# A hand-written issue order laid out anew: linear attention followed by a gated long convolution, on one core

## The chip, the cores and the metric

The kernel runs on one core of one Trainium2 chip. The metric is the device time of one execution in microseconds (us); three executions of the kernel before took 242.75, 243.77 and 244.01 us, so its median is 243.77 us. All computing engines of the core take part: TensorE (PE in the profile; PEld is its weight load), VectorE (DVE), ScalarE (ACT), GpSimd (POOL) and SyncE (SP), the last of which only issues transfers here.

## The reference

For each of 8 batches (b), 8 heads (h), 576 positions (s) and 64 channels (d), with inputs `q`, `k`, `v` of 9.4 MB each in float32:

```
kv  = einsum('bhsd,bhse->bhde', k, v)
out = einsum('bhsd,bhde->bhse', q, kv)
x   = out / sqrt(mean(out*out, -1) + 1e-6) * g_norm        # rows of 8*64 = 512 channels
x1, x2, x3 = split(x @ w_proj, 3)                          # each 576 x 512
x2c = irfft(rfft(x2, axis=time) * rfft(filter_fft, axis=time))
result = (x1 * x2c * x3) @ w_out                           # float32, (8, 576, 512)
```

## The kernel before, in words

Matrix operands are bfloat16 (the loads convert), sums are float32 in PSUM. The 576-point transform is done by matmuls with cosine and sine tables that the kernel makes itself. The sequence is folded into sums and differences first, so that short tables do.

**Steps.** The body is a set of named steps, and each step issues the instructions of one engine for one batch, with few exceptions. These are the ones that the text speaks of.

- Loads on POOL's queue: `Lq`, `Lk`, `Lv` bring one batch of an input (line 100; with `a` or `b` behind the name, half the heads), `Lf` the filter (L248), `Lw1`, `Lw2`, `Lw3`, `Lwo` the weights (L109). Input buffers are double.
- Set-up, once: `Z`, `Zi`, `Zt`, `Zf` make constants, `An0` to `An2` the tables `IV` (L176 to L183), `Tb0` to `Tb2` transpose them on PE, `Ff0` to `Ff2` fold the filter (L261, L263), `H0` to `H2` make the filter's spectrum `HH`, `HM` (L278 to L293), with ScalarE and VectorE taking turns. `Act` loads ScalarE's function table (L190). `W0_` to `W15_` are fillers: they put 4 matmuls on nothing (10 for `W0_`, L79) ahead of the next step that takes PSUM.
- Attention: `K` and `eK` make the kv blocks (L313, L319). `T0`, `T1` transpose q on PE for batches 0 and 1 (L340); from batch 2 on, `Qt` does that with a transposing DMA on SP's queue (L333). For each quarter j of the channels, `Oj` multiplies (L376), `sqj` squares and `obj` (or `ovj` on VectorE) scales out of PSUM (L386, L393, L391), `Rj` sums over a head (L383), `rsj` takes the inverse root (L397). `x0`, `x1` form the normalised x (VectorE, L409).
- Transform: `fd`, `fa`, `fr` fold x (VectorE, L420 to L434). `abM`, `abT`, `rrM`, `rrT` project the folded x by the middle third of w_proj (PE, L464, L471, L450, L457), `eab`, `eT`, `err` bring that to SBUF (ACT, L475). `F0`, `F1`, `F2` are the forward transform (L488 to L505).
- Product with the spectrum: `M0` and `M1` are two multiplications each on VectorE, a PSUM operand by an SBUF one, float32 into the SBUF tile `tpw` (L511, L512). `M2` is one (L527). Then the two halves of a complex product are added, both operands in SBUF: `Av1` on VectorE for group 1, `A0` on GpSimd for group 0 (both L518).
- Gates: for each quarter dc, `Gadc` and `Gbdc` project x by the first and last third of w_proj (PE, L537), `x1dc` copies the one out (ACT, L543), `gdc` multiplies the two (VectorE, L545).
- Inverse: `Io` and `I` for quarters 01 and 23 (PE, L561, L562; they read all that M2, A0 and Av1 of the batch wrote), `os` (ACT, L565), `u` (VectorE, L570, L571), `w` (L577 to L579), `fin` (L582, the product with the gates).
- Output: `U0`, `U2` and, every other batch, `U4` multiply by w_out (L609, L622), `ot0`, `ot2`, `ot4` copy out (ACT) and store with four DMAs each on SP (L616, L629). The last batch uses `V0` to `V3` (L641) with `va`, `vv` (L645, L648), in place of U0 and U2. Three output tiles are used in turn.

**What sets the order.** The kernel turns the framework's scheduler off: the written order of the steps is the order of each engine's queue. Three strings hold it. FIRST is done once, then ROUND for r = 0 to 6, then LAST. A `+` behind a step means the batch after r (`++` the second after), a `-` the one before; a step that was done already is left out. So a round runs a software pipeline: attention of batch r+2, transform and gates of batch r+1, the inverse's end of batch r and the output of batch r-1.

**PSUM.** There are four pairs of banks. `take` gives a step the pair that was freed longest ago in the written order, and the engine then waits until the step that freed it has really been done:

```
def take(key, n=2):
    i = min(range(4), key=lambda x: seen[x])
...
def free(key):
    seen[held.pop(key)] = clock[0]
```

So the written order sets not only the queues, it also sets which copy out of PSUM each matmul group waits for.

Of the kernel before, what the change touches and what calls it, by code (L numbers as in the profile page):

```python
# [16 lines left out]
MAGIC = 3.0 * (2.0 ** 22)  # L17


FIRST = """Lq Z Lkb Zi Zt An0 An1 An2 Zf Lf W0_ T1 W1_ Tb1 Tb0 Lvb Tb2 W10_ Ff0 T0 Lka Kb eTv1 Lva eKb O3 sq3 eTv0 Ff1 ov3 Ff2 O2 Ka  # L20
sq2 Act Lq+ W6_ R2 eKa ov2 rs2 W7_ O0 O1 Lk+ sq0 ov0 sq1 W8_ R3 rs3 W9_ H0 x1 R0 Lv+ rs0 W2_ W3_ T0+ W11_ R1 Lw2 ov1 eTa0+ rs1 fr1 fd1 x0
H1 fd0 T1+ fa0 fa1 fr0 K+ eK+ Lw1 H2 eTa1+ W4_ O0+ abM W5_ abT eab O1+ rrM eT F1 sq0+ sq1+ Lw3 rrT ob0+ Ga0 ob1+ err
M1 x10 R0+ Lwo F0 R1+ Ga1 rs0+ rs1+ x11 O2+ Gb0 Lv++ sq2+ Av1 F2 M0 ob2+ O3+ sq3+ Lq++ Gb1 g0 A0 ob3+ R2+ R3+
M2 rs2+ g1 x0+ Gb2 rs3+ x1+ Io01 os01 I01 Ga2 fd+ fa+ x12 Ga3 abM+ u01 g2 abT+ Gb3 w01 eab+ eT+ fr+ F1+ Io23
x13 rrM+ os23 g3 Lk++ rrT+ M1+ I23 F2+ u23 err+ F0+ M0+ w23 fin23 fin01"""

ROUND = """fd+ I23 fa+ Lq+++ Qt++ os23 fr+ ot0- Gb3 abM+ g3 rrM+ u23 K++ rrT+ eab+ U4- eK++ err+ w23 ot4- abT+ Ga1+ eT+
x11+ O3++ O2++ sq3++ sq2++ Lv+++ fin23 w01 ob3++ F1+ fin01 ob2++ U2- F0+ Ga0+ ot2- R2++ M1+ Gb0+ x10+ rs2++
M0+ O1++ Ga2+ g0+ sq1++ Av1+ ob1++ x12+ F2+ Lk+++ R3++ A0+ rs3++ O0++ Gb1+ M2+ sq0++ x1++ R1++ Gb2+ ob0++ g1+
rs1++ R0++ Io01+ g2+ rs0++ I01+ Ga3+ os01+ x0++ x13+ u01+ Io23+ U0"""  # L30

LAST = """os23 w01 ot0- I23 Gb3 U2- fin01 ot2- u23 g3 w23 fin23 U4 ot4 V3 V1 vv3 vv1 V0 V2 va2 va0"""


@with_exitstack
def kernel(
# [629 lines left out]
    def do(words, r):  # L666
        for word in words.split():
            n = word.rstrip("+-")
            b = r + word.count("+") - word.count("-")
            if 0 <= b < B and b in only.get(n, range(B)) and (n, b) not in did:  # L670
                clock[0] += 1
                step[n](b)
                did.add((n, b))

    do(FIRST, 0)
    for r in range(B - 1):
        do(ROUND, r)
    do(LAST, B - 1)

# [29 lines left out]
```

## Time and profile before

The profiled execution took 242.64 us; its span, from the first to the last instruction, is 240.9 us. So 1.7 us lie around the span, and the execution is 1.1 us below the median of 243.77 us.

| engine | busy, us | share of the span | instructions |
|---|---|---|---|
| PE | 215.6 | 89% | 1897 |
| VectorE | 203.5 | 84% | 323 |
| ScalarE | 150.8 | 63% | 236 |
| GpSimd | 45.9 | 19% | 55 |

The chain of waits that ended last is 60% PE and 26% VectorE. The granted TensorE clock is 0.991 over the span. Transfers move 30.14 MB, 125 GB/s on average, about 200 GB/s in the first 40 us.

How to read this: a share of busy time is an average over the start (to about 66 us), seven rounds of some 24 us, and the end. Within a round PE and VectorE are both almost always busy, so the question for any step is which of the two the other waits for at that place. A wait that several semaphores share is named after the one that came last.

### The profile page before, as it was taken

To read this page: it belongs to the slowest core of one execution; us is meant where nothing else is said; L and a number is where in the kernel's file an instruction comes from. 1 tells how busy PE (TensorE), PEld (TensorE's weight loads), DVE (VectorE), ACT (ScalarE), POOL (GpSimd) and SP (SyncE) were. 2 spreads that over 40 slices of the span, in tenths; PEclk is the share of its full clock that TensorE was granted. 3 is DMA by queue.
4 is the path that set the end of the run, shared out by engine and by line. 5 is a ranking of instruction groups with operands and counts; after the bars stand their busy time and mean duration, and the time that the engine had idled before them with its cause. 6 is when DMAs were issued, how large, how long until landed. Compare 5 with 4: busy or idle time off the path is not lost.

```text
span 240.9 us, 4753 instructions
## 1 busy us (share of the span) xinstructions
PE 215.6 (89%) x1897; PEld 126.6 (53%) x1897; DVE 203.5 (84%) x323; ACT 150.8 (63%) x236; POOL 45.9 (19%) x55
## 2 busy tenths in 40 slices
PE   7599997999979999799979997999799979997970
PEld 2354442466446755575547555755475557465520
DVE  3946288399999999999899999997999999999930
ACT  2648566884569558756875597568855875532421
POOL 7732000035043000700070007000300030003021
PEclk9999999999999999999999999999999999999996
DMA  5999999507999932997299819992703120430184
GB/s 47 198 198 204 206 206 176 102 1 105 203 185 135 162 90 44 167 189 171 68 171 189 186 35 175 172 191 64 165 3 87 24 65 1 104 93 25 42 214 140
DMA packets 41193, 30.14 MB, mean 125 GB/s; under 512 B 16050, under 2 KB 36530, under 8 KB 41170
## 3 DMA queue, kind: packets, MB, share of 16 engines
q0 software_dynamic: 21200, 17.11, 47.3%
q1 hardware_dynamic: 19778, 12.46, 22.6%
q8 instruction: 15, 0.25, 0.4%
q10 hardware_dynamic: 192, 0.26, 0.3%
q14 instruction: 8, 0.07, 0.1%
HBM read 33.69 MB, written 9.44 MB: 179 GB/s over the span
## 4 chain that ended last, share of the span: by engine, by line
PE 60%; DVE 26%; DMA 5%; ACT 3%; issue 2%; SPq 1%; ACTq 0%; DVEq 0%; POOLq 0%
PE ps L537 16%; PE ps L609 9%; DVE Y L518 8%; PE ps L464 4%; PE ps L561 4%; PE ps L79 3%; DVE Y L527 3%; DMA qb<-in_q_dram 3%; DVE g L545 3%; PE ps L471 3%; PE ps L450 3%; DVE tpw L512 2%; PE ps L313 2%; DVE tpw L511 2%; DMA out_dram<-ot 2%
## 5 line engine op out<-in xcount | busy, mean ns | idle before, releaser
L537 PE MATMUL ps<-x,wp 128*128 128x288 bf16 x512 | 72.7, 286 | 7.0 <-DVE Y L527 6.5
L537 PEld LDWEIGHTS <-wp 128*128 128x128 bf16 x512 | 47.3, 97 | 25.5 <-issue 11.6
L518 POOL TENSOR_TENSOR Y<-tpw 97x1024 bf16<-97x1024 f32 x8 | 18.8, 2352 | 164.4 <-DVE tpw L512 164.4
L475 ACT CAST x<-ps 128x1024 bf16<-128x1024 f32 (+1 forms) x24 | 20.6, 874 | 17.2 <-PE ps L464 14.7
L397 ACT ACTIVATE rstd<-ps,bias_eps 128x576 bf16<-128x576 f32 x32 | 23.8, 746 | 9.9 <-PE ps L383 9.8
L543 ACT CAST x<-ps 128x576 bf16<-128x576 f32 x32 | 20.5, 642 | 11.9 <-PE ps L537 10.3
L609 PE MATMUL ps<-wo,yg 128*128 128x512 bf16 x112 | 26.5, 379 | 0.0
L511 DVE TENSOR_TENSOR tpw<-ps,HH 128x1024 f32<-128x1024 f32 (+1 forms) x16 | 19.6, 1222 | 7.8 <-PE ps L498 7.2
L545 DVE TENSOR_TENSOR g<-ps,x 128x576 bf16<-128x576 f32 x32 | 23.3, 746 | 0.1
L386 ACT ACTIVATE sq<-ps 128x576 bf16<-128x576 f32 x32 | 20.0, 656 | 2.4 <-PE ps L376 2.3
L518 DVE TENSOR_TENSOR Y<-tpw 128x1024 bf16<-128x1024 f32 x8 | 20.6, 2571 | 0.0
L393 ACT ACTIVATE o<-ps,g_col 128x576 bf16<-128x576 f32 x28 | 20.1, 752 | 0.0
L79 PE MATMUL ps<-kvblk,ind 128*128 128x512 bf16 x54 | 16.5, 445 | 3.9 <-DVE ind L145 1.6
L512 DVE TENSOR_TENSOR tpw<-ps,HH 128x1024 f32<-128x1024 f32 (+1 forms) x16 | 19.4, 1214 | 0.0
L613 ACT COPY ot<-ps 128x1024 f32<-128x1024 f32 x14 | 14.2, 1015 | 7.6 <-PE ps L609 5.5
L561 PE MATMUL ps<-IV,Y 128*128 128x192 bf16 x128 | 16.5, 245 | 1.5 <-DVE Y L527 0.9
L609 PEld LDWEIGHTS <-yg 128*128 128x128 bf16 x112 | 10.6, 98 | 11.4
L565 ACT COPY os<-ps 128x576 f32<-128x576 f32 x16 | 10.2, 635 | 8.3 <-PE ps L562 5.7
L464 PE MATMUL ps<-wp,ab 128*128 128x512 bf16 x64 | 15.1, 379 | 0.0
L383 PE MATMUL ps<-sq,ind 128*128 128x288 bf16 x64 | 13.1, 286 | 0.8 <-ACT o L393 0.6
L409 DVE TENSOR_TENSOR x<-o,rstd 128x1152 bf16<-128x1152 bf16 x16 | 12.0, 750 | 1.5 <-ACT rstd L397 1.5
L561 PEld LDWEIGHTS <-Y 128*128 128x128 bf16 x128 | 10.3, 98 | 5.6 <-DVE Y L527 1.0
(135 smaller groups left out, 344.2 us busy)
## 6 DMA issues: line engine op xcount, KB each, us to landing
out_dram<-ot SPq DMA_DIRECT2D x56, 128.0 KB, 2.3
qb<-in_q_dram POOLq DMA_DIRECT2D x8, 576.0 KB, 8.1
kb<-in_k_dram POOLq DMA_DIRECT2D x7, 576.0 KB, 13.3
vb<-in_v_dram POOLq DMA_DIRECT2D x7, 576.0 KB, 10.3
wp<-in_moe_w_proj_dram POOLq DMA_DIRECT2D x3, 512.0 KB, 18.7
out_dram<-ot SPq DMA_DIRECT2D x24, 64.0 KB, 1.7
kb<-in_k_dram POOLq DMA_DIRECT2D x2, 288.0 KB, 9.1
fn<-in_moe_filter_fft_dram POOLq DMA_DIRECT2D x1, 576.0 KB, 8.4
```

Source lines behind the costliest of these rows:

```text
L79: nc.tensor.matmul(pair[i][:, 0], ind, kvblk[1].rearrange("p a b c -> p (a b c)"), start=True, stop=True)
L397: act.activation(out=by_time(rstd(), j), in_=by_row(tmp['r', b, j]), func=AF.Abs_reciprocal_sqrt, scale=1.0 / D, bias=bias_eps)
L464: nc.tensor.matmul(pp[:, h], abt()[:, j, h * SB:h * SB + P], w2(j), start=(j == 0), stop=(j == NDC - 1))
L475: act.copy(out=o_(), in_=tmp[key, b])
L511: vec.tensor_mul(out=t_[:n, 0], in0=xp[:n], in1=HH[:n, g, 1:3])
L512: vec.tensor_mul(out=t_[:n, 1], in0=xp[:n], in1=HH[:n, g, 0:2])
L518: op(out=Yt()[:n, 2 * g:2 * g + 2], in0=t_[:n, :, 0], in1=t_[:n, :, 1])
L537: nc.tensor.matmul(pp[:, h, 0:TH], w_, x[:, j, h * TH:(h + 1) * TH], start=(j == 0), stop=(j == NDC - 1))
L543: act.copy(out=x1, in_=pp[:, :, 0:TH])
L545: vec.tensor_mul(out=halves(g13t()[:, dc]), in0=pp[:, :, 0:TH], in1=x1)
L561: nc.tensor.matmul(pp[:, i, 0:SB], Y[:, 2 * g + h, cs], IV[:, 2 * g + h, 0:SB], start=(g == 1), stop=(g == 2))
L609: nc.tensor.matmul(pp[:, cc], ygt(b)[:, dc, c * P:(c + 1) * P], wo[:, dc], start=(dc == 0), stop=(dc == NDC - 1))
```

## The change

Only the three strings are changed; no step is added or altered, except that fewer fillers are named (W0, W1, W2, W6 to W9 and W12 in place of W0 to W11). In the set-up, the filter's load goes ahead of k and v, both transposes of q ahead of the tables, `Act` ahead of `Zt`, and `F0` with `M0` of a batch comes before `M1` in batch 0 and 1. In a round, `A0` is written behind `M0` and ahead of `M2`, `g0`, `g1` and `Av1`. In LAST the final inverse follows the last gates.

```
-ROUND = """fd+ I23 fa+ Lq+++ Qt++ os23 fr+ ot0- Gb3 abM+ g3 rrM+ u23 K++ rrT+ eab+ U4- eK++ err+ w23 ot4- abT+ Ga1+ eT+
-x11+ O3++ O2++ sq3++ sq2++ Lv+++ fin23 w01 ob3++ F1+ fin01 ob2++ U2- F0+ Ga0+ ot2- R2++ M1+ Gb0+ x10+ rs2++
-M0+ O1++ Ga2+ g0+ sq1++ Av1+ ob1++ x12+ F2+ Lk+++ R3++ A0+ rs3++ O0++ Gb1+ M2+ sq0++ x1++ R1++ Gb2+ ob0++ g1+
-rs1++ R0++ Io01+ g2+ rs0++ I01+ Ga3+ os01+ x0++ x13+ u01+ Io23+ U0"""
+ROUND = """K++ Lk+++ x0+ Qt++ U0- Lq+++ x13 eK++ fd+ Io23 u01 O2++ fa+ Gb3 fr+ ot0- Lv+++ os23 I23 abM+ g3 sq2++ u23
+ob2++ rrM+ eab+ abT+ rrT+ eT+ U4- O1++ w01 err+ ot4- sq1++ ob1++ O3++ sq3++ fin01 ob3++ F1+ U2- w23 fin23 F0+
+ot2- M1+ Ga1+ x11+ F2+ Ga0+ M0+ Gb0+ x10+ A0+ R3++ M2+ O0++ Gb1+ g0+ R2++ rs3++ Ga2+ g1+ sq0++ Av1+ ob0++
+rs2++ R0++ x1++ Gb2+ x12+ R1++ rs0++ rs1++ g2+ Ga3+ Io01+ os01+ I01+"""
...
-LAST = """os23 w01 ot0- I23 Gb3 U2- fin01 ot2- u23 g3 w23 fin23 U4 ot4 V3 V1 vv3 vv1 V0 V2 va2 va0"""
+LAST = """u01 Io23 x13 U0- I23 w01 U2- os23 u23 fin01 ot0- Gb3 w23 ot2- g3 fin23 V2 V1 U4 va2 vv1 V3 V0 ot4 vv3 va0"""
```

FIRST, before and after:

```
-FIRST = """Lq Z Lkb Zi Zt An0 An1 An2 Zf Lf W0_ T1 W1_ Tb1 Tb0 Lvb Tb2 W10_ Ff0 T0 Lka Kb eTv1 Lva eKb O3 sq3 eTv0 Ff1 ov3 Ff2 O2 Ka
-sq2 Act Lq+ W6_ R2 eKa ov2 rs2 W7_ O0 O1 Lk+ sq0 ov0 sq1 W8_ R3 rs3 W9_ H0 x1 R0 Lv+ rs0 W2_ W3_ T0+ W11_ R1 Lw2 ov1 eTa0+ rs1 fr1 fd1 x0
-H1 fd0 T1+ fa0 fa1 fr0 K+ eK+ Lw1 H2 eTa1+ W4_ O0+ abM W5_ abT eab O1+ rrM eT F1 sq0+ sq1+ Lw3 rrT ob0+ Ga0 ob1+ err
-M1 x10 R0+ Lwo F0 R1+ Ga1 rs0+ rs1+ x11 O2+ Gb0 Lv++ sq2+ Av1 F2 M0 ob2+ O3+ sq3+ Lq++ Gb1 g0 A0 ob3+ R2+ R3+
-M2 rs2+ g1 x0+ Gb2 rs3+ x1+ Io01 os01 I01 Ga2 fd+ fa+ x12 Ga3 abM+ u01 g2 abT+ Gb3 w01 eab+ eT+ fr+ F1+ Io23
-x13 rrM+ os23 g3 Lk++ rrT+ M1+ I23 F2+ u23 err+ F0+ M0+ w23 fin23 fin01"""
+FIRST = """Z Lq Lf Zi Lka Act Zt Lva An0 An1 An2 Lvb W0_ T1 Zf T0 eTv0 eTv1 Tb0 Lkb Lq+ Lw2 Ff2 Ff0 Tb2 Ff1 W2_ Ka eKa W1_ Tb1 O1 sq1
+ov1 O0 sq0 R0 rs0 W6_ R1 Kb eKb rs1 ov0 O2 sq2 ov2 W7_ O3 Lk+ R2 sq3 R3 rs2 x0 rs3 ov3 x1 Lv+ fr1 T0+ fr0 T1+ eTa0+
+Lw1 eTa1+ H2 H0 rrM fd0 rrT fa0 fd1 err fa1 W8_ H1 F0 W9_ abM eab K+ M0 eK+ abT O2+ eT sq2+ O0+ F2 sq0+ F1 ob2+ Lw3
+ob0+ O3+ M2 sq3+ Lwo ob3+ M1 R2+ Ga0 Lq++ rs2+ Ga1 R3+ R0+ x10 Gb0 x11 O1+ A0 Av1 rs3+ rs0+ g0 Gb1 sq1+ ob1+
+Lk++ R1+ x1+ Ga3 Ga2 g1 Io01 rs1+ Gb3 x13 Lv++ x0+ fr+ x12 os01 I01 rrM+ rrT+ fd+ fa+ g3 err+ abT+ eT+ Io23
+u01 os23 I23 abM+ F0+ eab+ Gb2 F2+ u23 M0+ F1+ g2 M1+ w23 fin23 w01 fin01 K++ Lk+++ Qt++ Lq+++ eK++ W12_ O2++"""
```

## The prediction

> **What bounds the kernel now.** I read the page's busy times first, then the timeline of one round engine by engine, then the stages one by one, then the end.
>
> ```profile
> PE 215.6 (89%) x1897; PEld 126.6 (53%) x1897; DVE 203.5 (84%) x323; ACT 150.8 (63%) x236; POOL 45.9 (19%) x55
> ...
> DVE  3946288399999999999899999997999999999930
> ```
>
> PE and VectorE are both nearly full from 46 us on, so neither share says which one rules. The timeline of one round does:
>
> ```profile
> 119.70 1.21 DVE L512 TENSOR_TENSOR tpw<-ps,HH 97x1024 f32<-97x1024 f32 x1
> 120.83 0.75 DVE L545 TENSOR_TENSOR g<-ps,x 128x576 bf16<-128x576 f32 x1
> 121.50 3.02 DVE L518 TENSOR_TENSOR Y<-tpw 128x1024 bf16<-128x1024 f32 x1
> 124.44 1.21 DVE L527 TENSOR_TENSOR Y<-ps,HM 128x1024 bf16<-128x1024 f32 x1
> ```
>
> ```profile
> 121.09 2.35 POOL L518 TENSOR_TENSOR Y<-tpw 97x1024 bf16<-97x1024 f32 x1 [19.98 <-DVE tpw L512]
> ```
>
> ```profile
> 125.71 1.14 PE L537 MATMUL ps<-x,wp 128*128 128x288 bf16 x8 [1.27 <-DVE Y L527]
> ```
>
> GpSimd's sum (A0) starts 0.18 us behind M0's second product and runs to 123.44. VectorE's sum (Av1) starts at 121.50 and takes 3.02 us; its end, 124.52, is A0's end and 1.08 us. M2 (L527) follows late, and PE waits 1.27 us for the pair that M2 frees (Gb2). That is PE's only marked gap of a round. The first batch shows each piece alone:
>
> ```profile
> 48.64 1.22 DVE L518 TENSOR_TENSOR Y<-tpw 128x1024 bf16<-128x1024 f32 x1
> ...
> 52.05 0.74 DVE L545 TENSOR_TENSOR g<-ps,x 128x576 bf16<-128x576 f32 x1
> 52.72 1.21 DVE L527 TENSOR_TENSOR Y<-ps,HM 128x1024 bf16<-128x1024 f32 x1
> ...
> 69.75 2.44 DVE L578 TENSOR_TENSOR w<-u,w 128x384 bf16<-128x384 bf16 x1
> ```
>
> ```profile
> 52.22 2.36 POOL L518 TENSOR_TENSOR Y<-tpw 97x1024 bf16<-97x1024 f32 x1 [28.59 <-DVE tpw L512]
> ```
>
> Av1 without A0 takes 1.22 us. A0 beside products that read PSUM (52.05, 52.72) takes the same 2.36 us, and these take their usual 0.74 and 1.21. The next A0 (batch 1) hits L578, whose two inputs lie in SBUF: 2.44 us, where its median is 0.36. So A0 stops VectorE's work from two SBUF operands, not its PSUM products.
>
> **A round, worked out.** Rounds last 23.79 us, 24.58 with U4 (stage table, from U2 to U2):
>
> ```profile
> 115.88:139.67 23.79, 22.51 (x212) 13.97 (x211) 22.86 (x31) 16.60 (x27) 4.62 (x4) 1.00 0.83 151
> 139.67:164.25 24.58, 23.30 (x219) 14.36 (x218) 22.87 (x31) 17.40 (x28) 4.61 (x4) 1.00 0.83 146
> ```
>
> The columns are length, then busy PE, PEld, DVE, ACT, POOL. PE is busy 22.51 and idle 1.28. In the new order VectorE does M1, M0, M2, g0, g1, Av1. A0 starts 0.18 us behind M0 and needs 2.35 us; M2, g0 and g1 take 1.13 + 0.67 + 0.67 = 2.47 us start to start. So Av1 meets at most 0.1 us of A0 and falls from 3.02 to 1.22, and VectorE's load falls by 1.8 to 21.05 us. Av1's unknown price lies between 1.22 and 3.02; I take 1.22, because the order leaves A0 only PSUM products as company.
>
> What is late next? I walked the new order with these durations, time 0 being K's start. PE has K 0.78, U0 1.73, Io23 0.43, O2, Gb3, I23, abM 1.73, rrM 0.95, abT 0.96, rrT, O1, O3 and so on; F1 starts at 9.2, U2 10.06, F0 11.8, Ga1 12.4, F2, Ga0, Gb0 15.05, Gb1 16.55, Ga2 17.85, Gb2 19.15, Ga3, and the inverse ends at 22.3. The releases come before each: eT 9.0 for F1, err 9.95 for U2, ob3 12.2 for Ga1, M1 13.0 for Ga0, M2 16.5 for Gb1, g1 18.4 for R0, rs0 20.3 for Io01. VectorE's own loop, from rs1 over x0, fd, u01, fa, fr, g3, u23, w01, fin01, w23, fin23, M1, M0 and M2 (17.3 us), then Gb1 to R1 on PE (4.1) and rs1 (0.75), is 22.2 us, with hand-overs 22.3. So PE's 22.5 rules, by a margin of 0.2 us only. I take 1.2 us saved in each of the five rounds that show the full wait (101.1 to 197.9): **6.0**, with ends 3.0 (half goes to hand-overs) and 6.4. In batch 7 PE waits 0.60 and 0.88 us for Av1 and M2 (220.1, 221.2); in the new order ten gate groups lie between F1 and Io01, and Av1 is done 1 us early: **1.3** saved (1.0 to 1.5).
>
> POOL's three loads stand ahead of A0; they are issued right behind the last A0, wait for nothing that is late, and land in 8.1 to 13.4 us (medians), while their readers come over 20 us later. Qt is moved behind ot2's stores on SP, see the rivals.
>
> **The start.** Up to I01 of batch 1 I walked the order in the same way. q lands at 9.03 before, with half of k behind it; now the filter (576 KB) is second. At the rates of the transfer rows q lands between 9.0 and 10.6 us; I take 9.1, as the rows show q done when 0.81 MB had moved. Both transposes (12 take 1.14 us cold) end at 11.4, the angle tables at 11.6 as before, and Tb0, Ff2, Ff0, Tb2, Ff1 and Ka follow to 17.3. From there the two orders compare so (us):
>
> | | before, row | after, worked out |
> |---|---|---|
> | x complete for batch 0 | 34.7 | 27.5 |
> | first spectrum product (M1, now M0) | 46.25 | 38.7 |
> | Ga0 of batch 0 | 46.7 | 44.8 |
> | K of batch 2 | 67.2 | 61.9 |
> | M2 of batch 1 | 76.1 | 68.6 |
> | I01 and Ga3 of batch 1 done | 80.5 | 75.6 |
>
> What moves the first product is the H steps: with ScalarE and VectorE taking turns at 1.5 us per pair, they come when x is folded already, and F0 needs only the rr part. The gain shrinks again, since VectorE then waits some 4 us for F2, Gb0, Gb1 and F0. My hops are about 0.09 us short each (an O group starts its square 0.36 us after its own start, I counted 0.25 and 0.1), on some 14 hops of the path: 1.2 us. So **3.7** of the 4.9 remain. Ends: 0 (q at 10.6 and twice the hop error) and 5.5. Hidden costs: two more function table loads (1.28 each) run before ScalarE's first input at 4.3 us; the one ahead of rs0 takes the place of the one at 21.91. The 16 fillers taken away are 0.22 us each when warm, and lay in gaps.
>
> **The end.** From I01 of batch 7 to the last fin is 6.85 us before (222.97 to 229.82). After, VectorE has only g2 beside Io01 and os01, so the path is os01, u01, w01, u23, fin01, w23, g3, fin23: 7.6 us, **0.75 lost**. Behind fin the stores take 11.1 us now (to 240.9); with V2 and V1 ahead of U4, and the last tile waiting only for V1's stores, I get 10.4: **0.7 gained**, uncertain by 1 us either way.
>
> **Sum.** 6.0 + 1.3 + 3.7 - 0.75 + 0.7 = 10.95 us of the profiled 242.64, so 231.7 for that execution; the median lies 1.1 above it: **232.8 us**.
>
> **Rivals.**
>
> *Hand-overs eat the round* (0.13). The margin of 0.2 us is thin, as the next release is late wherever one copy is. Half of the rounds' gain (3.0), 1.3, and 2 of the start: 6.3 saved, 237.5 us. For it: both loops are within 1%. Against: the old order shows no gap but one.
>
> *A0 still meets Av1* (0.06), so the change doesn't do what it says: if POOL's loads hold A0 back by 2 us, Av1 waits as now and only the start pays, 240.1, or 243.8 if that gives nothing either (half each). Against: POOL shows no wait before its loads in the rounds.
>
> *Qt comes late* (0.07), the slower side. Now Qt is issued at 121.20 or 144.56 and its readers, the O matmuls, run 17 to 18 us later (138.36, 163.08). In the new order Qt follows ot2's stores (15.9 in the round before), and O2 of that batch is at 2.9: 9.3 us later. It takes 5.1 us to land, 8.5 at most. From 9.3 us on PE, in order, stops at O2 with Gb3, I23 and abM behind it, and each further us counts in five rounds. At 3 us beyond, 15 us are lost against 11 gained: 248 us. For it: k, q and v of the next batch are issued 2 us behind it and share the transfer engines. Against: that was so before.
>
> *PE falls to its slow pitch in the start* (0.04). Four fillers take 1.91 us at 9.98 and 1.04 at 14.66, so PE was slow until about 12 us, after an idle stretch of 3 us. My walk leaves no gap over 1.4 us after that. If one slow stretch of 2.9 us came back, half of it is lost: 234.2. The Trainium skill, "TensorE: Matmul & The Clock Gate", section "What's actually happening", says that an idle window of about 3.4 us takes the clock to half, which speaks against dropping fillers; by the gaps of my walk it would not happen.
>
> *The forecast* has 0.70, its own range 229.4 to 235.5.
>
> **Range and chances.** The low end takes all upper ends (6.4, 1.5, 5.5 and +1 at the end: 229.4). The high end takes in the hand-over case with nothing from the start and a worse end: 238.5. About 0.5% (1.2 us) is what a measurement can tell from no change. Faster: 0.70 + 0.13 + 0.04 + 0.03 = 0.90; same: 0.03; slower: 0.07.
>
> **What would show it.** Av1 at 1.2 us in every round, A0 beside L527 and L545; no PE wait for L527; rounds of 22.5 to 22.7 (23.3 with U4); M0 of batch 0 near 40; the span behind fin23 near 10.4 us. Wrong if PE shows waits over 0.3 us for L475, L527 or Qt's data in each round, or if the first product comes after 45 us.

## The result and the profile after

The new kernel takes 232.47 us (median of four executions, 230.74 to 234.36), the kernel before, run beside it, 243.26 us (242.37 to 244.01). The ratio is 0.953, with a 95% interval of 0.945 to 0.962. The profiled execution took 231.38 us, with a span of 229.6. A ratio compares undisturbed executions only, so it need not be the quotient of the two medians.

The page of the new kernel, busy times and VectorE's tenths:

```profile
PE 209.0 (91%) x1860; PEld 126.4 (55%) x1881; DVE 191.7 (83%) x323; ACT 152.3 (66%) x238; POOL 45.8 (20%) x55
...
DVE  4864587789898999899889998998899989998920
```

VectorE lost 11.8 us of busy time with the same 323 instructions, so single instructions became shorter: 10.9 us of it is Av1, whose eight instances took 20.6 us before and take 9.7 now. The timeline of one round shows which (VectorE, then GpSimd; columns as before: start, duration, engine, line, operation):

```profile
91.25 1.22 DVE L512 TENSOR_TENSOR tpw<-ps,HH 97x1024 f32<-97x1024 f32 x1
92.38 1.22 DVE L527 TENSOR_TENSOR Y<-ps,HM 128x1024 bf16<-128x1024 f32 x1
93.67 0.76 DVE L545 TENSOR_TENSOR g<-ps,x 128x576 bf16<-128x576 f32 x1
95.18 0.76 DVE L545 TENSOR_TENSOR g<-ps,x 128x576 bf16<-128x576 f32 x1 [0.75 <-PE ps L537]
95.86 1.22 DVE L518 TENSOR_TENSOR Y<-tpw 128x1024 bf16<-128x1024 f32 x1
```

```profile
92.64 2.35 POOL L518 TENSOR_TENSOR Y<-tpw 97x1024 bf16<-97x1024 f32 x1 [24.11 <-PE ps L537]
94.94 0.79 POOL L100 DMA_DIRECT2D kb<-in_k_dram  x1
```

A0 now runs from 92.64 to 94.99, beside M2 and g0. Av1 starts behind it, at 95.86, and takes 1.22 us instead of 3.02. Two rounds of the new kernel, each from one F2 to the next (length, then busy PE, PEld, DVE, ACT, POOL); measured so, the rounds of the kernel before are 24.59 and 23.78 us:

```profile
90.79:113.95 23.16, 23.05 (x218) 14.59 (x218) 21.22 (x32) 17.22 (x27) 4.61 (x4) 1.00 0.87 160
113.95:136.25 22.30, 22.19 (x210) 14.14 (x210) 21.05 (x32) 16.62 (x26) 4.63 (x4) 1.00 0.90 155
```

A round is 1.44 to 1.48 us shorter, and PE is now busy in all but 0.11 us of it. So PE bounds the rounds, and the wait for L527 is gone from them.

Where the 11.3 us of span went (240.9 less 229.6), at the same places in both traces:

| stretch | before | after | saved | predicted |
|---|---|---|---|---|
| start, until I01 and Ga3 of batch 1 are through PE | 80.48 | 77.21 | 3.27 | 3.7 |
| from there to the same of batch 7 | 142.49 | 133.35 | 9.14 | 6.0 + 1.3 |
| from there to fin23's end | 6.85 | 7.70 | -0.85 | -0.75 |
| from fin23's end to the span's end | 11.1 | 11.34 | -0.25 | +0.7 |

The table compares one execution of each kernel. The rounds repeat to 0.02 us in the other profile of the new kernel, but the first row is 2.8 us larger there and the last 0.8 us smaller (see the slow pitch and the end, below).

### The profile page after: what moved, and what is told of

Same layout as the page of the kernel before. It is cut to its first block, busy times and chain, and to the rows that moved or that the text cites. A ratio compares the mean times of both kernels' runs of the same rounds, so it can differ in the third digit from the quotient of the medians.

```text
span 229.6 us, 4731 instructions
## 1 busy us (share of the span) xinstructions
PE 209.0 (91%) x1860; PEld 126.4 (55%) x1881; DVE 191.7 (83%) x323; ACT 152.3 (66%) x238; POOL 45.8 (20%) x55
## 4 chain that ended last, share of the span: by engine, by line
PE 72%; DVE 15%; ACT 6%; issue 2%; DMA 2%; POOL 1%; ACTq 0%; DVEq 0%; POOLq 0%
PE ps L537 26%; PE ps L609 9%; PE ps L464 5%; PE ps L561 4%; PE ps L383 3%; PE ps L471 3%; PE ps L450 3%; PE ps L313 2%; PE ps L376 2%; PE ps L261 2%; PE ps L505 2%; PE ps L497 2%; DMA out_dram<-ot 2%; PE ps L457 1%; PE ps L490 1%
## 5 line engine op out<-in xcount | busy, mean ns | idle before, releaser
L537 PE MATMUL ps<-x,wp 128*128 128x288 bf16 x512 | 71.3, 286 | 0.6 <-ACT o L393 0.5
L537 PEld LDWEIGHTS <-wp 128*128 128x128 bf16 x512 | 49.0, 98 | 17.1 <-issue 1.1
L545 DVE TENSOR_TENSOR g<-ps,x 128x576 bf16<-128x576 f32 x32 | 24.0, 754 | 5.3 <-PE ps L537 5.1
L386 ACT ACTIVATE sq<-ps 128x576 bf16<-128x576 f32 x32 | 21.0, 662 | 1.7 <-PE ps L376 1.7
L511 DVE TENSOR_TENSOR tpw<-ps,HH 97x1024 f32<-97x1024 f32 (+1 forms) x16 | 19.5, 1220 | 2.0 <-PE ps L498 1.3
L393 ACT ACTIVATE o<-ps,g_col 128x576 bf16<-128x576 f32 x28 | 21.1, 758 | 0.0
L512 DVE TENSOR_TENSOR tpw<-ps,HH 97x1024 f32<-97x1024 f32 (+1 forms) x16 | 19.4, 1215 | 0.0
L561 PE MATMUL ps<-IV,Y 128*128 128x192 bf16 x128 | 16.2, 245 | 0.0
L565 ACT COPY os<-ps 128x576 f32<-128x576 f32 x16 | 10.3, 642 | 7.1 <-PE ps L562 6.1
L570 DVE TENSOR_TENSOR u<-ps,os 128x576 bf16<-128x576 f32 x16 | 12.0, 750 | 1.8 <-ACT os L565 1.8
L562 PE MATMUL ps<-IV,Y 97*128 97x96 bf16 x64 | 13.2, 207 | 0.0
L79 PE MATMUL ps<-kvblk,ind 128*128 128x512 bf16 x35 | 11.5, 452 | 1.8 <-DVE ind L145 1.6
```

The costliest lines, as they stand in the source:

```text
L386: act.activation(out=halves(sq()[:, j]), in_=tmp['o', b, j][:, :, 0:TH], func=AF.Square)
L393: act.activation(out=by_time(osb(), j), in_=i_, func=AF.Copy, scale=g_col)
L511: vec.tensor_mul(out=t_[:n, 0], in0=xp[:n], in1=HH[:n, g, 1:3])
L537: nc.tensor.matmul(pp[:, h, 0:TH], w_, x[:, j, h * TH:(h + 1) * TH], start=(j == 0), stop=(j == NDC - 1))
L545: vec.tensor_mul(out=halves(g13t()[:, dc]), in0=pp[:, :, 0:TH], in1=x1)
L561: nc.tensor.matmul(pp[:, i, 0:SB], Y[:, 2 * g + h, cs], IV[:, 2 * g + h, 0:SB], start=(g == 1), stop=(g == 2))
```

## The experiments

### Is it A0 beside a sum of two SBUF operands?

The new kernel with one step moved: Av1 directly behind M2, so in the middle of A0.

```
-... M0+ Gb0+ x10+ A0+ R3++ M2+      O0++ ... Ga2+ g1+ sq0++ Av1+ ob0++
+... M0+ Gb0+ x10+ A0+ R3++ M2+ Av1+ O0++ ... Ga2+ g1+ sq0++      ob0++
```

> The new kernel with Av1 written right behind M2 in the rounds, ahead of g0 and g1, so that it falls into the middle of A0. Theory (A0 stops VectorE's work from two SBUF operands, and keeping them apart is what the rounds gained): Av1 takes about 2.5 us (1.4 us of waiting for A0 and 1.1), g0 comes 2 us late, PE's R2 waits for g0's pair by about 2 us in each of six rounds, total about 243 to 245 us. Rival (the gain comes from the new order of the PSUM releases, A0 does not matter): Av1 stays at 1.22 us, R2 waits about 0.6 us, total 235 to 237 us.

Measured: 244.46 us (243.31 to 247.15), ratio 1.006 [1.002, 1.009]: the whole gain is gone. VectorE of this kernel, GpSimd, and PE behind it:

```profile
120.72 1.21 DVE L527 TENSOR_TENSOR Y<-ps,HM 128x1024 bf16<-128x1024 f32 x1
121.85 2.55 DVE L518 TENSOR_TENSOR Y<-tpw 128x1024 bf16<-128x1024 f32 x1
124.32 1.41 DVE L545 TENSOR_TENSOR g<-ps,x 128x576 bf16<-128x576 f32 x2
```

```profile
120.97 2.35 POOL L518 TENSOR_TENSOR Y<-tpw 97x1024 bf16<-97x1024 f32 x1 [20.36 <-PE ps L537]
```

```profile
125.12 0.40 PE L383 MATMUL ps<-sq,ind 128*128 128x288 bf16 x2 [1.65 <-DVE g L545]
```

A0 ends at 123.32. Av1 ends at 124.40, that is A0's end and 1.08 us, the same as in the kernel before. The product L527, which also ran beside A0, took its 1.21. What VectorE loses delays the products behind Av1: PE waits 1.65 us for g in a round (2.00 in two later ones). Start and end are written as in the new kernel, so this one placement decides.

### The part alone, in the kernel before

Only Av1 (and x1, which may not come ahead of it) is moved, behind g1.

```
-M0+ O1++ Ga2+ g0+ sq1++ Av1+ ob1++ ... M2+ sq0++ x1++ R1++ Gb2+ ob0++ g1+
+M0+ O1++ Ga2+ g0+ sq1++      ob1++ ... M2+ sq0++      R1++ Gb2+ ob0++ g1+ Av1+ x1++
```

> The kernel before with Av1 and x1 written behind g1 in the rounds, nothing else. Theory: Av1 falls from 3.02 to 1.22 us, M2 comes early and PE's wait of 1.27 us for it goes; about 0.5 us of it comes back as a wait of Io01 for Av1, so five rounds gain some 0.9 us and the last batch about 1: total 237 to 239 us. Rival (the PSUM releases): no change, 243 us within 1.

Measured: 241.76 us (240.76 to 243.62), ratio 0.994 [0.991, 0.997]. Av1 takes 1.21 us, and the wait for L527 is gone, yet a round (24.27 with U4, 23.47 without) is only 0.31 us shorter. PE in one of its rounds:

```profile
127.04 0.34 PE L561 MATMUL ps<-IV,Y 128*128 128x192 bf16 x2 [0.58 <-DVE Y L518]
128.37 1.14 PE L537 MATMUL ps<-x,wp 128*128 128x288 bf16 x8 [0.31 <-DVE g L545]
```

The stall moved. The inverse (L561) needs Av1, which is now the last step ahead of it, and Ga3 needs the pair that g1 frees. The theory (237 to 239 us) had the mechanism right and the size wrong: it had the wait of the inverse, but not that of Ga3 behind it, nor the 0.17 us that each wait costs beyond what it shows (see the table of rounds below).

The next kernel moves Ga3 ahead of the inverse as well, to give Av1 time:

```
-rs1++ R0++ Io01+ g2+ rs0++ I01+ Ga3+ os01+
+rs1++ R0++ Ga3+ Io01+ g2+ rs0++ I01+ os01+
```

> The kernel before with Av1 and x1 written behind g1 (as in e2) and Ga3 ahead of Io01. Theory (e2 gained only 0.31 us a round because PE then waited 0.58 us at Io01 for Av1, each wait costing 0.17 more than it shows): Ga3's 1 us covers that wait, rounds of 22.7 to 22.8 us (23.5 with U4), total 237 to 239 us. Rival (the four PSUM pairs in their new rotation bring another wait of the same size): 241 to 243 us as e2.

Measured: 240.72 us (239.54 to 242.19), ratio 0.989 [0.986, 0.992]; rounds of 23.85 and 23.04, 0.74 us shorter than before; the total lies between the theory and the rival. The wait for Av1 is gone and another has come, since the order of takes decides which pair the inverse gets:

```profile
128.85 0.32 PE L561 MATMUL ps<-IV,Y 128*128 128x192 bf16 x2 [0.51 <-DVE g L545]
```

### GpSimd's sum given to VectorE

The kernel before, and the new one, each with the sum of group 0 on VectorE; what is computed is the same.

```
-summ(b, g, nc.gpsimd.tensor_add)
+summ(b, g, vec.tensor_add)
```

> The kernel before with the sum of group 0 on VectorE instead of GpSimd, order unchanged. Theory: in the old order GpSimd's sum costs VectorE 1.81 us per round (2.08 in batch 1) and saves it 1.13, so doing it on VectorE is faster: rounds shorter by 0.6 to 0.7 us, total 238 to 240 us. Rival (GpSimd's sum relieves VectorE): 1.1 us more per round, total 249 to 251 us.

> The new kernel with the sum of group 0 on VectorE. Theory (PE's own work of 22.3 us rules a round, VectorE's loop is within 0.2 us of it): 1.13 us more on VectorE lengthens its loop past PE's and each of seven rounds by about 1.0 us, total 239 to 240 us. Rival (PE rules with room to spare): 232.5 to 233.5 us.

In the kernel before: 240.86 us (239.7 to 241.8), ratio 0.991 [0.987, 0.995], so less of a gain than the 238 to 240 expected. Both sums now take 1.21 us, so VectorE, with more to do, is faster: Av1 loses 1.81 us and A0 adds 1.13 start to start, 0.68 net, and a round is 0.71 us shorter. In the new order, where A0 already costs VectorE nothing, the same edit costs: 237.69 us (237.3 to 240.41), ratio 0.982 [0.977, 0.987], and 0.88 to 0.90 us per round, where 1.0 and a total of 239 to 240 were expected. VectorE's loop grew by 1.13, so its margin to PE was about 0.24 us; the prediction had 0.2. The wait that shows it:

```profile
119.86 1.14 PE L537 MATMUL ps<-x,wp 128*128 128x288 bf16 x8 [0.83 <-DVE Y L527]
```

### The start alone

The kernel before with the new FIRST:

> The kernel before with the new FIRST, ROUND and LAST as before. Theory: the start's gain stands by itself, 3.3 us by the traces, total about 240 us. Rival (the new FIRST gains only together with the new ROUND, which takes up its state): 243 us or more.

Measured: 241.29 us (240.57 to 243.56), ratio 0.994 [0.990, 0.998]. F2 of batch 2 comes at 95.56 instead of 97.20, so 1.6 of the 3.27 us stand without the new ROUND. That is between the theory and the rival. The rest probably needs both, as FIRST's last part is laid out for the new round's first steps, but no run shows it, and this profile too is one execution with a slow start (see the slow pitch, below).

### The last batch's order

The new kernel with the old LAST (with the four steps that the new ROUND leaves to it):

```
-LAST = "u01 Io23 x13 U0- I23 w01 U2- os23 u23 fin01 ot0- Gb3 w23 ot2- g3 fin23 V2 V1 U4 va2 vv1 V3 V0 ot4 vv3 va0"
+LAST = "u01 Io23 x13 U0- os23 w01 ot0- I23 Gb3 U2- fin01 ot2- u23 g3 w23 fin23 U4 ot4 V3 V1 vv3 vv1 V0 V2 va2 va0"
```

> The new kernel with the last batch's steps in the old LAST's order (u01, Io23, x13 and U0 written ahead of it). Theory: the new LAST gained nothing, since behind Io01 the path runs through VectorE's chain and the stores either way (fin23 7.7 us behind the last gates and 11.3 us of stores, against 6.85 and 11.1 before): 232.5 us within 1. Rival (the V steps ahead of U4 save 0.7 us of stores, as predicted): 233.2 us or more.

Measured: 231.17 us (230.56 to 233.92), ratio 0.956 [0.951, 0.960], against 0.953 for the new kernel in its first runs, and 230.86 us for it on the chip of this one (below). Three executions have a span of 228.7 or 228.8 us, as the shortest of the new kernel have: the new LAST brings nothing that can be measured. In both orders Gb3 and g3 come behind I23, so the inverse follows the last gates only in its first half. Behind fin23 lie 11.34 us in the new kernel's profile, most of it stores and copies that wait for an output tile, on ScalarE:

```profile
223.91 0.58 ACT L645 COPY ot<-ps 128x512 f32<-128x512 f32 x1 [2.51 <-DMA out_dram<-ot]
```

So I tried to take that wait away: the last four tiles go to the idle buffers `tpw`, and the stores of V1 go out on GpSimd's queue and those of V0 on ScalarE's instead of half on SP. In the last round Io01 and I01 stand ahead of Ga3. The new kernel itself ran beside it, unchanged but for an empty line.

```
-        ot = ot_tile()
+        ot = buf("tpw", c % 2, [P, 2, 2, DM], FP32)[:, c // 2]
...
-            (q1 if i >= 2 else nc.sync).dma_start(...)
+            (q1 if i >= 2 or c < 2 else nc.sync).dma_start(...)
...
-        do(ROUND, r)
+        do(ROUND if r < B - 2 else ROUND.replace("Ga3+ Io01+ os01+ I01+", "Io01+ os01+ I01+ Ga3+"), r)
```

> The new kernel unchanged, timed again beside the next two on one chip: 231 to 233.5 us, about 0.953 of the kernel before. No theory is at stake; it is the base for the next kernel.

> The new kernel with two edits at its end: the four V tiles lie in the idle tpw tiles (so no copy waits for an output tile) and all stores of vv1 go to POOL, all of va0 to ACT, while SP keeps half of va2 and vv3; and in the last round Io01 and I01 are written ahead of Ga3. Theory (behind the last fin the stores wait for output tiles, 1.5 and 2.5 us, and then queue on SP): the last copy 1.3 us earlier, the span behind fin23 9 to 9.5 us instead of 11.3, the last fin 0.4 us earlier; total 2 to 3 us less than the new kernel. Rival (the transfers themselves, at some 2.3 us each on shared engines, end the kernel): 0.5 us less at most.

Measured: the new kernel again 230.86 us (230.54 to 234.28), ratio 0.948 [0.943, 0.952]; the variant 234.65 us (233.01 to 236.73), ratio 0.963 [0.957, 0.968], so slower. The last copy does come earlier (222.88 instead of 223.91), but SP's queue of stores is held up. The other edit did not pay either: with Io01 ahead of Ga3 the inverse waits 0.46 us for Av1, and fin23 ends 15.54 us behind F2 of batch 7, against 15.08 in the new kernel. SP's first and last issues at the end, of the new kernel and of the variant:

```profile
214.11 4.22 SPq L616 DMA_DIRECT2D out_dram<-ot  x8
...
225.27 1.83 SPq L648 DMA_DIRECT2D out_dram<-ot  x4
```

```profile
214.37 7.50 SPq L616 DMA_DIRECT2D out_dram<-ot  x8
...
227.49 0.85 SPq L648 DMA_DIRECT2D out_dram<-tpw  x2
```

And what the variant's SP queue waited for in that stretch:

```profile
SPq L616 <- DMA out_dram<-tpw: 3.4, 1, 3.4
SPq L629 <- DMA out_dram<-tpw: 2.8, 1, 2.8
```

Seven stores of the batch before go out, the eighth waits 3.4 us, by the trace for the landing of a store from `tpw`, of which ScalarE had issued the first two at 219.87, and fewer stores on SP end later than more did. Neither theory had that. Why a store on one queue should wait for one on another isn't settled; releasers are inferred.

### The slow pitch in the start

In the new kernel PE folds the filter (L261) at half its speed: a group of four follows the one ahead at 0.43 us, while the last ones (16.85 is 0.22 behind 16.63), and all of the kernel before (where they lie at 15.6 and 19.1), follow at 0.22.

```profile
13.23 0.91 PE L261 MATMUL ps<-fn,rev 96*32 96x512 bf16 x4
13.65 0.91 PE L261 MATMUL ps<-fn,ident 96*32 96x512 bf16 x4
...
16.85 0.55 PE L261 MATMUL ps<-fn,rev 96*32 96x512 bf16 x4
```

Three kernels change only fillers, whose results nothing uses. First 7 more ahead of q, then none at all:

```
-tmp.update(warm=tmp.get("warm", 0) + (4 if n else 10))
+tmp.update(warm=tmp.get("warm", 0) + (4 if n else 17))
...
+tmp.update(warm=0)
```

> The new kernel with 17 instead of 10 filler matmuls ahead of the first transposes, so that PE has hardly a gap before q lands at 8.8 us. Theory (the slow pitch of PE from 12.2 to 16.3 us in the new kernel's profile follows from the idle stretch of 2.8 us before it, and costs the start): no slow stretch after 9 us, the first Ka and what follows 1 to 2 us earlier, total 230.5 to 231.5 us. Rival (the stretch is hidden behind the k and v loads and ScalarE's chain): the slow stretch goes, the total stays at 232.5 us within 0.5.

> The new kernel without any filler matmuls. Theory (fillers keep PE at its fast pitch): PE is slow until some 4 us after q lands and again after gaps of the start, the start takes 2 to 4 us longer, total 234 to 237 us. Rival (the 38 fillers only fill): 232.5 us within 0.7, or less by the time that fillers stood in the way of real work.

With 7 more: 231.51 us (228.82 to 233.49; the kernel before, beside it, 242.59). The profiled execution still has the slow stretch, from 12.3 to 17.3. But the executions fall in two groups: three with a clock of 0.975 to 0.980 and spans of 230.8 to 231.6 (the profiled one is among them), three with 0.992 to 0.997 and spans of 226.8 to 227.9. No execution of the new kernel was above 0.983 or below 228.7. With none: 231.94 us (231.15 to 233.58), ratio 0.957 [0.954, 0.961]; the slow stretch lasts from q's arrival (8.8) to 16.2, and the page's clock tenths (one digit for 5.75 us) show another from 23 to 34 us, and K of batch 2 comes at 64.96, against 63.80 in the new kernel's profile. So both slow stretches of the theory came, but not its 234 to 237 us; the total is the rival's, and how much of the slow time the missing fillers give back was not separated:

```profile
PEclk9999558999999999999999999999999999999998
```

That pointed at the gaps rather than at the total of fillers. The last kernel closes both gaps: 16 fillers more ahead of q, and 4 ahead of the first table transposes.

```
-... T0 eTv0 eTv1     Tb0 Lkb ...
+... T0 eTv0 eTv1 W3_ Tb0 Lkb ...
...
-tmp.update(warm=tmp.get("warm", 0) + (4 if n else 10))
+tmp.update(warm=tmp.get("warm", 0) + (4 if n else 26))
```

> The new kernel with 26 instead of 10 fillers ahead of the first transposes of q (16 more, to about 8.7 us) and 4 fillers more between these and the first table transposes (about 9.9 to 10.8); nothing else differs. In the new kernel's profile the granted clock is 0.82 from 9 to 10 us, 0.50 from 10 to 16 and 0.77 from 16 to 17, behind a stretch in which TensorE was idle for 2.8 us; with 7 fillers more the idle stretch was 1.85 us, the fall to 0.50 came at 11.2 in the profiled execution, and three of six executions had a clock of 0.992 to 0.997 and spans of 226.8 to 227.9. Theory: the slow stretch follows a spell of little TensorE work ahead of it, so covering both gaps (7 to 8.8 and 10.3 to 11.5) keeps the clock at 1.00 from 5 to 17 us in most executions: filter matmuls at a pitch of 0.22 instead of 0.43, x of batch 0 complete near 27.5 instead of 29.3, spans near 227 and a median of 229 us, in the rounds no difference. Rival: the slow stretch comes whatever PE did before it (it came in every start profiled so far); then the median stays at 230.9 to 232.5 with a clock of 0.97 to 0.98, or 0.5 us above if fillers delay the transposes of q. Third: the start is full speed but the gain is lost again to VectorE's waits before the rounds; then x comes at 27.5 and the span stays near 228.7.

Measured: 228.83 us (228.59 to 230.35), ratio 0.941 [0.937, 0.945], so the theory's time and below the rival's. All six executions have a clock of 0.989 to 0.997 and spans of 226.8 to 228.6; the eleven of the new kernel have 0.965 to 0.983 and 228.7 to 232.6. The start of the new kernel and of this one (length, busy PE, PEld, DVE, ACT, POOL, then the granted clock):

```profile
5.00:7.00 2.00, 1.06 (x3) 0.15 (x1) 1.83 (x7) 0.45 (x3) 2.00 (x4) 1.00 1.14 146
7.00:9.00 2.00, 0.17 (x4) 0.17 (x5) 1.90 (x5) 1.71 (x5) 1.97 (x3) 1.00 1.21 214
9.00:12.00 3.00, 2.23 (x31) 1.66 (x28) 2.59 (x21) 2.16 (x5) 0.94 (x2) 0.61 1.12 196
12.00:17.00 5.00, 5.00 (x44) 2.54 (x44) 3.28 (x7) 1.89 (x3) 2.87 (x4) 0.55 1.31 202
```

```profile
5.00:7.00 2.00, 2.00 (x6) 0.73 (x5) 1.83 (x7) 0.30 (x2) 2.00 (x4) 1.00 1.11 138
7.00:9.00 2.00, 2.00 (x9) 0.83 (x8) 1.90 (x5) 1.72 (x5) 2.00 (x3) 1.00 1.24 216
9.00:12.00 3.00, 2.94 (x34) 1.91 (x34) 2.61 (x21) 2.19 (x5) 0.79 (x1) 1.00 1.10 198
12.00:17.00 5.00, 4.95 (x69) 2.64 (x70) 3.21 (x8) 3.08 (x4) 2.86 (x4) 1.00 1.31 202
```

The filter's groups now follow at 0.22:

```profile
12.99 0.59 PE L261 MATMUL ps<-fn,ident 96*32 96x512 bf16 x4
13.21 0.58 PE L261 MATMUL ps<-fn,rev 96*32 96x512 bf16 x4
```

Both kernels are busy from 12 to 17, but the new one gets 44 matmuls through where this one gets 69. The fillers even delay q's transposes, from 8.83 to 10.10, and still x of batch 0 is complete at 27.72 instead of 29.26, the first product comes at 38.78 instead of 40.32, and K of batch 2 at 62.26 instead of 63.80. The 1.54 us pass through the start and the rounds whole, to the end of fin23 (216.73 instead of 218.26). The span is 2.3 us shorter; the other 0.77 lie behind fin23, in the stores (10.57 us instead of 11.34). This is the fastest kernel of the study.

The new kernel can lose more than 1.54 us. Its second profile, of an execution with a span of 231.6 us, has these clock tenths (one digit for 5.8 us):

```profile
PEclk9758998899999999999999999999999999999998
```

A second fall lies at 38 to 44 us (granted clock 0.81, 0.50 and 0.84 in three stretches of 2 us), behind an idle gap of 1.29 us; the first profile has the same gap there and a clock of 1.00. In this execution the first product comes at 41.45 and K of batch 2 at 66.61, 4.35 us later than with both gaps closed. The profile with 7 fillers more has the second fall too. The order of the start before is not free of this: in the kernel with Av1 and Ga3 moved, whose FIRST is the old one, K of batch 2 comes at 68.88, against 67.24 in the profile of the kernel before. So the 3.27 us that the start saved hold for one pair of executions, and the medians mix several.

## Why the prediction was right, point by point

**A0 against Av1: right, and shown.** Av1 at 1.22 us in every round as forecast; one move of it in the new order brings the old time back. The Trainium skill, "SBUF — State Buffer", section "SBUF: two separate sides", says that a VectorE operation with two SBUF inputs and a GpSimd one that reads SBUF lock each other out for a whole instruction; the trace agrees (Av1 2.55 or 3.02 us beside A0 and 1.22 without, products from PSUM 1.21 in both cases).

**"PE's 22.5 rules, by a margin of 0.2 us": the margin was right, the two times were not.** 1.2 us per round was too little: it is 1.44 to 1.48. The mis-sized term is PE's busy time of 22.51. A matmul of 288 columns lasts 0.286 us in the trace, but eight of them take 1.14 us, so each starts 0.122 behind the one ahead. When PE must wait, the last one's remaining 0.16 to 0.17 us still counts as busy, and the shown wait starts only behind it. A round costs 22.30 us by starts alone, and each wait costs what it shows and 0.17. The 22.30 is the new kernel's own round, so the last row is no test; five of the other six agree within 0.06 us, and one is 0.12 off:

| kernel | waits shown in a round without U4 | 22.30 and (wait + 0.17) each | measured |
|---|---|---|---|
| before | 1.27 | 23.74 | 23.78 |
| Av1 beside A0 | 1.65 | 24.12 | 24.11 |
| Av1 moved alone | 0.58, 0.31 | 23.53 | 23.47 |
| no GpSimd sum, old order | 0.57 | 23.04 | 23.08 |
| Av1 and Ga3 moved | 0.51 | 22.98 | 23.04 |
| no GpSimd sum, new order | 0.83 | 23.30 | 23.18 |
| new | none | 22.30 | 22.30 |

VectorE's loop, put at 22.3, was too long by about the same 0.2: by its margin of 0.24 it is near 22.06. That the margin came out right is luck of two equal errors. The rounds and batch 7 together saved 9.14 us instead of 7.3: from F2 of batch 2 to F2 of batch 7 it is 7.12 for 6.0, and the other 0.7 lie ahead of that and behind it and were not separated.

**The hand-overs did not eat the round, but they could have.** In the old order, taking the collision away brought 0.31 to 0.74 us per round of 1.48, as the next release was late each time. The rival (half of the gain) fits these kernels, and the new ROUND escapes it.

**The start: 3.27 against 3.7, and the deduction behind it was wrong.** My walk had x of batch 0 at 27.5, the first product at 38.7 and K of batch 2 at 61.9; I then took 1.2 us off for hops. With the slow stretch removed, the chip gave 27.72, 38.78 and 62.26, and I01 and Ga3 of batch 1 done at 75.67 for 75.6, so the walk had needed a third of that at most. What the new kernel lost instead is 1.54 us by the slow pitch (in the profiled execution), the fourth rival, which was given 0.04 and 1.45 us. The step that failed is "my walk leaves no gap over 1.4 us after that": the gap that mattered lies ahead of q (2.77 us), and the new order puts the filter's matmuls into the slow stretch that follows it, where the kernel before had four fillers and the transposes of the tables (9.98 to 14.7). The two errors nearly cancel, which is luck, and 0.04 was too little for a rival that came in both profiles of the new kernel. The rule that the prediction cited from the Trainium skill, "TensorE: Matmul & The Clock Gate", section "What's actually happening", was weighed against the wrong gaps. Its direction is borne out by the clock column above; its idle window of about 3.4 us was not needed here as one gap: 2.77 us ahead of q were followed by a fall, and so were 1.85 us (with 1.26 more at 10.3) in three of six executions, by their clock and spans, and 1.29 us at 37.4 in the second profile.

**Qt: right.** It is issued at 92.50 and lands 5.1 us later, its first reader starts at 102.72, and PE shows no wait for it.

**The end: -0.75 was right (-0.85), +0.7 did not come (-0.25).** The step that failed is "the last tile waiting only for V1's stores": the new order has the same three output tiles, and the last copy waits 2.51 us for one of them. The size itself is not settled by one execution: six other profiles that end like the new kernel have 10.5 to 10.9 us behind fin23, and five that end like the kernel before have 11.1 to 12.7. But the new kernel with the old LAST has 10.55 as well, so the order of LAST is not what shortens it; what does is open.

In sum, terms of the wrong size offset each other: +1.8 in the rounds and batch 7, -0.4 in the start, -1.1 at the end. 11.3 us were saved of 10.95 forecast, so that the total came out this close is in part luck. The stated high end of 238.5 does not follow from its terms: with 3.0 and 1.3 saved and nothing from the start it is 239.5 before any worse end.

## What to carry to other kernels

Look at single durations, not at shares: an instruction that takes 3.02 us in each round and 1.22 us once names its own cause. Taking a collision away frees only what the next release lets through, so an order must be walked to the next late hand-over before its gain is priced, and each wait priced with the drain of the matmul ahead of it. Where a start is laid out anew, ask which matmuls fall behind PE's idle stretches, not only how long these are, and profile more than one execution before a gain of 1 or 2 us is put down to the order.

## What the runs showed of the hardware that was not expected

- Three loads issued on GpSimd's queue (0.77 to 0.80 us each, 94.94 to 97.25) ran beside Av1 (95.86 to 97.08) without slowing it: 1.22 us. It is the sum that blocks, not the queue's work.
- The clock column can stay silent. In the kernel without fillers it shows 1.00 from 12 to 17 us while the filter's groups follow at 0.43 us; the pitch of equal matmuls is the safer reading. The profile of the kernel before (1.00, and four fillers in 1.91 us at 9.98) and that of the new kernel with the old LAST (1.00, and 40 matmuls from 12 to 17 us) have the same; the mean clock of the latter is 0.992, with a span of 229.7. Across the executions of the new kernel the mean clock went with the span: 0.983 with 228.7 to 228.9, 0.974 to 0.976 with 229.1 to 229.6, 0.965 to 0.968 with 231.4 to 232.6.
- From PE's first work the slow pitch lasted 7.4 us in the kernel without fillers (8.8 to 16.2), and 3.3 us (1.6 to 4.9) in the profiled execution with 7 fillers more. So it has no fixed length from the first matmul on.
- With stores spread over three queues, eight issues on SP took 7.50 us instead of 4.22 (4.83 in the kernel with both gaps closed). Why is open.
